# An mLSTM and soft-MoE kernel: q and k tiles on 128 partitions, gate rows as 4096-byte rows, and a newly written instruction order

## The chip, the cores and the metric

The kernel runs on one core of a Trainium2 chip. The metric is the device time of one execution in microseconds (us); lower is better.

## The reference, cut to what matters

The input has 4 batches, 8 heads, 768 positions and 40 values per head. First comes a gated linear attention with a running state per head, written as a recurrence in time:

```
m_new = max(f_gate + m, i_gate); f_stab = exp(f_gate + m - m_new); i_stab = exp(i_gate - m_new)
C = f_stab * C + i_stab * outer(v, k);  n = f_stab * n + i_stab * k
y = sigmoid(o_gate) * (C q) / max(|n.q|, 1)
```

Its result, as 3072 rows of 320 values, goes through one feed-forward layer and then through a soft mixture of experts:

```
h = x @ w_in;  x = (h * sigmoid(h)) @ w_out              # 320 -> 2048 -> 320
logits = x @ phi;  d = softmax of logits over the 3072 rows (per slot, 32 slots)
slot_input = d.T @ x;  per expert e (8): slot_out = relu(slot_input[e] @ w1[e]) @ w2[e]     # 320 -> 1024 -> 320
c = softmax of logits over the 32 slots;  out = c @ slot_out
```

## The kernel before, in words

The recurrence is computed in chunks. A tile is 128 positions of one batch with all 8 heads; there are 24 tiles, and two tiles make a block of 256 rows, of which there are 12. For each tile the kernel loads q and k (`load_qk`), k and v in rows (`load_v`), the gate rows (`rows`, from the scratch tensor `md` in device memory) and, for two tiles at once, the output gate (`load_o`). TensorE then makes the scores (`sc`, L610), the state update (`st`, L643) and the output (`pv`, L669), and turns the output round (`xT`, L689). `qs` multiplies q by a gate row into `xq`; `mask`, `arg` and `exp` make the decay weights; `vw` weighs v. Each block goes through the feed-forward layer in eight steps (`mlp.blk.q`: 16 matmuls at L716, then a Silu on ScalarE at L718), and its hidden values are turned by VectorE (`gU`, L725) into two tiles named `g`. The logits (`lg`, L735; `lsum`, L747) and the slot sums (`slots`, L775, two steps of 32 matmuls, one for each `g` tile of the block) follow.

Ahead of this, the weights `w_in` (`load_wi`, `load_wr`) and `w_out` (`load_wo`) come in a 64-bit layout and are converted on ScalarE and VectorE (`wi`, `wr`, `wo`); the converted `w_out` is turned round and multiplied by phi (`wpT`, L450; `wp`, L462). After the last block come the slot inputs (`slot_in`), the two expert layers (`s1`, L932, which needs all tiles of `w1`; `s2`, L959, which needs `w2`) and the output (`out`, L977, and its transfers at L981). The steps `warm` and `heat` are matmuls whose results nobody reads.

The order of all work is the string `ORDER`: a list of 1416 tokens such as `mlp.3.6` or `load_w2.2.3`. Each token issues the next step of the operation it names; each engine works through its steps strictly in this order. `ENG` says which engine does a step that several could do. All loads but those of the last stage's output go through the one queue of SyncE, also in this order: a load that must wait for its buffer holds up all loads behind it.

Memory is reused. The tiles of the attention lie in a pool that `free_at` closes, and 10 of the 20 tiles of `w1` are then loaded over it. Five more are loaded into the common buffers `cv` in the earlier blocks. The tiles of the feed-forward layer lie in a pool that `free_mp` closes, and the 32 tiles of `w2` (320 KB each) and the last five of `w1` (512 KB each) are loaded over that. By the code, that pool holds per partition eight weight tiles of 4096 bytes, `wr` with 8192, `gT` with 16384, then the four buffers of `g` with 8192 bytes each (at 57344, 65536, 73728 and 81920), then the block's inputs. The tile `w2_e_k` lies at byte (8k + e) x 2560, so `load_w2.2.3` (e = 2, k = 3) at 66560 lies in the second buffer of `g`, `load_w2.6.3` at 76800 in the third, and the first tile of `load_w1.6` at 81920 in the fourth:

```
for k in range(4):
    for e in range(NE):
        w2t[e, k] = yp.tile([128, 2, DM], F32, name=f"w2_{e}_{k}")
for e, c in ((6, 0), (6, 1), (6, 2), (7, 0), (7, 1)):
    w1t[e, c] = yp.tile([128, F2], F32, name=f"w1_{e}_{c}")
```

A load into such a tile waits only for the readers of what lay there.

Of the kernel before, what the change touches and what calls it, by code (L numbers as in the profile page):

```python
# [78 lines left out]
load_wo.4 xT.0 wi.3 wi.3 pv.1 load_v.2 vw.2 xT.0 xT.0 st.2 rows.2 pv.1 pv.1 xT.1 wi.3 wi.3 wo.4 xT.1 xT.1 mlp.0.0 wo.4 wo.4 load_wo.0 load_wo.2 sdec.1.1
load_wo.3 wi.3 wo.2 wo.2 wo.0 wo.0 wo.2 wo.0 sadd.1.1 wo.3 wo.3 mask.2 arg.2 exp.2 wo.3 decay.0 mlp.0.0 mlp.0.5 mlp.0.5 load_qk.2 sc.2 sw.2 load_wo.1 wo.1  # L80
wo.1 wo.1 decay.0 load_wo.14 wo.14 wo.14 wo.14 load_wo.7 wo.7 wo.7 wo.7 mlp.0.2 mlp.0.2 load_wo.13 wo.13 wo.13 wo.13 load_wo.6 wo.6 wo.6 wo.6 wpT.1 wpT.0
mlp.0.4 mlp.0.4 mlp.0.7 mlp.0.6 load_wo.15 wo.15 wo.15 load_wo.5 wpT.0 wo.15 wo.5 wo.5 wo.5 wpT.1 load_wo.12 wo.12 wo.12 wo.12 mlp.0.7 load_wo.10 wpT.3 wo.10
wo.10 wpT.2 mlp.0.6 wpT.3 wo.10 sdec.2.0 sadd.2.0 load_wo.11 wo.11 wo.11 wpT.2 mlp.0.3 load_p load_wo.9 wo.9 wo.9 wo.9 load_wo.8 wo.8 wo.8 wo.8 wo.11 wpT.6
wpT.6 wpT.7 mlp.0.1 wpT.7 load_v.3 mlp.0.1 sdec.2.1 wpT.4 wpT.4 mlp.0.3 wpT.5 wpT.5 qs.2 pv.2 mask.3 gU.0.0 load_o.1 sadd.2.1 sdec.3.0 wz.0 wpT.8 vw.3 wz.1
gU.0.0 wpT.9 sig.1 wpT.8 wpT.9 st.3 sadd.3.0 pv.2 rows.3 arg.3 exp.3 sdec.3.1 sadd.3.1 gU.0.1 pv.2 pv.2 wp load_qk.3 wp sc.3 sw.3 qs.3 xT.2 xT.2 wp wp
load_qk.4 sc.4 xT.2 pv.3 pv.3 pv.3 lg.0 mask.4 load_v.4 vw.4 pv.3 xT.3 st.4 gU.0.3 lg.0 load_o.2 lsum.0 xT.3 xT.3 rows.4 arg.4 exp.4 sw.4 mlp.1.0 mlp.1.0
load_v.5 lsum.0 vw.5 mlp.1.1 rows.5 mlp.1.1 qs.4 sdec.4.0 sadd.4.0 pv.4 sig.2 lsum.0 row.0 gU.0.1 mlp.1.2 mlp.1.2 mlp.1.5 gU.0.2 pv.4 load_v.6 gU.0.2 mlp.1.5
pv.4 row.0 gU.1.0 lsum.0 load_qk.5 qs.5 mlp.1.4 sdec.4.1 gU.0.3 pv.4 sadd.4.1 mlp.1.4 xT.4 xT.4 mlp.1.6 mlp.1.6 gU.1.0 mask.5 st.5 sdec.5.0 sadd.5.0 arg.5
exp.5 sc.5 gU.1.2 sw.5 lsum.0 mlp.1.7 mlp.1.7 mlp.1.3 mlp.1.3 vw.6 init row.0 pv.5 pv.5 xT.4 pv.5 pv.5 lg.1 lg.1 row.0 row.0 slots.0 load_qk.6 rows.6 sdec.6.0
mask.6 xT.5 rows.8 xT.5 load_v.7 load_w1.0 load_w1.0 slots.0 arg.6 exp.6 xT.5 mlp.2.1 mlp.2.1 mlp.2.3 gU.1.1 gU.1.1 slots.0 slots.0 slots.0 slots.0 row.0  # L90
# [982 lines left out]
```

## Time and profile before

| what | us |
|---|---|
| time, median of 3 runs | 413.08 (411.52 to 414.05) |
| time of the profiled execution | 412.9 |
| its span, first to last instruction | 411.1 |
| PE busy in the span | 388.4 (94%) |
| DVE, ACT, POOL busy | 247.3, 241.1, 119.9 |

The span is what the trace covers; the rest of the time lies around it. Engines: PE is the TensorE matmul, PEld its weight load, DVE is VectorE, ACT is ScalarE, POOL is GpSimd, and SPq is the queue of loads on SyncE.

### The profile page before, as it was taken

What the parts mean: (1) busy time and instruction counts of PE and PEld (TensorE: products, weight loads), DVE (VectorE), ACT (ScalarE), POOL (GpSimd) and SP (SyncE); (2) the same over time, 40 slices, a digit from 0 to 9 for tenths busy, and PEclk for the clock granted to TensorE, in tenths of its full rate; (3) what the DMA queues carried; (4) which work ended last, traced back from release to release, by engine and by line L of the source; (5) the groups of instructions that cost most, each with busy time, mean ns of one, the idle gap of its engine ahead of it and who ended that gap; (6) DMA issues with size and microseconds to landing.
All of it is one profiled execution on the core that took longest, in us unless ns stands there. A gap on an engine that the chain in (4) does not pass through costs nothing.

```text
span 411.1 us, 14943 instructions
## 1 busy us (share of the span) xinstructions
PE 388.4 (94%) x6526; PEld 316.9 (77%) x6526; DVE 247.3 (60%) x569; ACT 241.1 (59%) x475; POOL 119.9 (29%) x169
## 2 busy tenths in 40 slices
...
GB/s 255 346 260 281 232 274 226 117 214 216 250 78 237 155 84 157 164 104 172 167 195 57 127 70 242 111 157 183 157 96 65 77 357 290 204 279 364 227 135 251
DMA packets 36992, 78.43 MB, mean 191 GB/s; under 512 B 3616, under 2 KB 18656, under 8 KB 36288
## 3 DMA queue, kind: packets, MB, share of 16 engines
...
## 4 chain that ended last, share of the span: by engine, by line
PE 74%; DMA 15%; DVE 3%; SPq 3%; issue 2%; ACT 1%; POOL 1%; DVEq 0%; ACTq 0%; POOLq 0%
PE h L716 39%; DMA w<-in_moe_w 6%; PE w L669 5%; PE t L735 5%; PE w L775 5%; DMA qk<-in_qk 5%; PE w L610 3%; PE w L643 3%; PE t L959 3%; DMA mq<-md 2%; PE t L689 2%; PE h L238 2%; PE t L395 1%; DMA cv<-in_moe_w_out 1%; PE t L747 1%
## 5 line engine op out<-in xcount | busy, mean ns | idle before, releaser
L718 ACT ACTIVATE gT<-h 128x512 f32<-128x512 f32 x96 | 56.4, 598 | 63.3 <-PE h L716 59.2
L716 PE MATMUL h<-xh,wh 128*128 128x256 f32 x384 | 83.0, 298 | 1.0 <-ACT gT L718 1.0
L716 PE MATMUL h<-xl,wh 128*128 128x256 f32 x384 | 77.4, 283 | 0.0
L716 PE MATMUL h<-xh,wl 128*128 128x256 f32 x384 | 77.3, 283 | 0.0
L725 DVE STREAM_TRANSPOSE g<-gT 128x512 f32<-128x512 f32 x96 | 63.5, 690 | 12.6 <-ACT gT L718 12.6
L716 PEld LDWEIGHTS h<-xh,wh 128*128 128x128 f32 x384 | 59.4, 191 | 11.7 <-issue 3.4
L716 PEld LDWEIGHTS h<-xh,wl 128*128 128x128 f32 x384 | 59.7, 191 | 0.0
L716 PEld LDWEIGHTS h<-xl,wh 128*128 128x128 f32 x384 | 59.6, 191 | 0.1
L716 PE MATMUL h<-xh,wr 128*128 128x256 f32 x192 | 54.3, 283 | 0.0
L716 PE MATMUL h<-xl,wr 128*128 128x256 f32 x192 | 54.2, 282 | 0.0
L594 POOL TENSOR_TENSOR xq<-qk,mq 104x512 f32<-104x512 f32 x20 | 25.7, 1286 | 44.6 <-ACT mq L303 16.3
L779 DVE SCALAR_TENSOR_TENSOR acc<-acc,vec,w 128x512 f32<-128x512 f32 x44 | 30.1, 737 | 11.6 <-PE w L775 11.6
L716 PEld LDWEIGHTS h<-xl,wr 128*128 128x128 f32 x192 | 36.8, 192 | 0.0
L716 PEld LDWEIGHTS h<-xh,wr 128*128 128x128 f32 x192 | 36.8, 192 | 0.0
L718 ACT ACT_TABLE_LOAD x27 | 34.6, 1283 | 1.9 <-DVE g L725 1.4
L570 POOL TENSOR_TENSOR arg<-mq,arg 128x512 f32<-128x512 f32 x17 | 22.8, 1339 | 20.1 <-DVE arg L564 11.8
L775 PE MATMUL w<-g,et 32*32 32x512 f32 x768 | 27.4, 600 | 0.1
L654 DVE TENSOR_TENSOR vb<-vb,w 104x164 f32<-104x164 f32 x40 | 12.6, 314 | 24.1 <-PE w L643 17.0
L669 PE MATMUL w<-vb,xq 40*64 40x41 f32 x768 | 24.4, 227 | 1.2 <-issue 1.2
L669 PE MATMUL w<-kv,xs 64*64 64x41 f32 x768 | 24.9, 229 | 0.0
L618 DVE TENSOR_TENSOR xs<-w,arg 128x512 f32<-128x512 f32 x24 | 16.4, 683 | 13.2 <-ACT arg L575 6.6
L669 PEld LDWEIGHTS w<-kv,xs 64*64 64x64 f32 x768 | 20.7, 133 | 4.4 <-issue 1.8
...
## 6 DMA issues: line engine op xcount, KB each, us to landing
...
rawi<-in_moe_w_in SPq DMA_DIRECT2D x4, 1024.0 KB, 12.0
...
```

Source lines behind the costliest of these rows:

```text
L570: eng(f"arg.{n}", "G" if n else "V").tensor_tensor(out=arg, in0=mb.rearrange("p r (c t) -> p r c t", c=2), in1=arg, op=ALU.add)
L594: eng(f"qs.{n}", "G").tensor_tensor(out=xq[LR], in0=qkt[n % 2][LR, 0:4], in1=st[n]["qb"][LR], op=ALU.mult)
L610: T_.matmul(sc[64 * z:64 * z + 64, y, f:f + 64], qkn[o:o + D, 4 + p, t], qkn[o:o + D, 8 * y + x, t], start=True, stop=True, tile_position= ...
L618: V_.tensor_tensor(out=h2(d["xs"]), in0=d["sc"], in1=h2(d["arg"]), op=ALU.mult)
L654: V_.tensor_tensor(out=dst, in0=dst, in1=u, op=ALU.add)
L669: T_.matmul(op[64 * ch:64 * ch + 64, NP * par + p], a, vv[k][r, ch, p], start=(k == 0), stop=(k == 1), tile_position=(o, 64 * ch))
L716: T_.matmul(hp[:, z], w, x, start=(y == 0), stop=(y == 7))
L718: A_.activation(out=gt[0][:, 2 * q:2 * q + 2], in_=hp, func=AF.Silu)
L725: V_.transpose(out=us[blk][a][:, :, 4 * q:4 * q + 4].rearrange("p b c f -> p c b f"), in_=gt[0][:, 4 * q:4 * q + 4, 128 * a:128 * a + 128] ...
L735: T_.matmul(lp[32 * j:32 * j + 32], wp[:, j, 32 * q:32 * q + 32], gt[0][:, 4 * q + j], start=(q == 0), stop=(q == 3), tile_position=(0, 32 ...
L775: T_.matmul(ap[g][32 * b:32 * b + 32], d["et"][p, 4 * a + b], u[p, b].rearrange("p c f -> p (c f)"), start=(a == 0), stop=(a == 1), tile_p ...
L779: V_.scalar_tensor_tensor(out=acc[:, g], in0=acc[:, g], scalar=al[:, blk:blk + 1], in1=ap[g], op0=ALU.mult, op1=ALU.add)
```

## The change

Four things change, and no step is added or taken away: both orders hold the same 1416 tokens, each as often.

- q and k are loaded on 128 partitions, where it was 112 before (partitions 40 to 63 and those from 104 on hold zeros): 640 KB instead of 560 KB a tile.
- `md` lies so that the two gate rows of a pair of heads stand side by side. The two transfers of `rows` stay two, each to 64 partitions and of 256 KB, but a partition's data is one row of 4096 bytes where it was two of 2048. The tile `mq` is laid out likewise, so its readers read runs of 128 values with a step.
- The pads behind the rows of `qk` and `kv` in device memory are gone.
- `ORDER` and `ENG` are written anew, for the buffers as the program builds them.

```diff
-DP = 112
+DP = 128
...
-load_f scan first load_c keys keys mask.0 rest first load_o.0 sig.0 decay.1 prow.1 prow.1 rest rest rest load_wr wr wr wr mb0 rest decay.1 decay.1 wr wr
...
-free_at load_w1.4 load_w1.4 pv.23 load_w1.4 load_w1.2 mlp.10.5 mlp.10.5 row.9 row.9 row.9 mlp.10.2 mlp.10.2 gU.10.1 xT.23 mlp.10.4 slots.9 load_w1.2 load_w1.2
...
-lsum.10 lsum.10 load_w1.3 mlp.11.0 mlp.11.0 gU.11.0 free_mp load_w2.1.0 mlp.11.3 mlp.11.3 load_w2.0.0 lsum.10 load_w2.2.0 mlp.11.2 load_w2.4.0 mlp.11.2
-load_w2.3.0 row.9 row.9 row.10 load_w2.5.0 gU.10.3 gU.10.2 gU.10.3 mlp.11.7 mlp.11.7 gU.11.0 lsum.10 slots.10 load_w1.6 mlp.11.6 load_w2.2.1 load_w1.6
-mlp.11.6 gU.11.3 mlp.11.5 row.10 gU.10.2 mlp.11.5 mlp.11.4 mlp.11.4 load_w2.3.1 row.10 load_w1.7 gU.11.1 gU.11.1 gU.11.2 slots.10 load_w2.2.3 lg.11 lg.11
-slots.10 slots.10 slots.10 lg.11 lg.11 lg.11 lsum.11 load_w2.7.0 slots.10 lsum.11 heat.6 load_w2.4.1 load_w1.6 lsum.11 load_w1.7 heat.2 load_w2.7.1
-load_w2.5.1 lsum.11 lsum.11 slots.11 load_w2.6.3 before before load_w2.4.3 gU.11.2 gU.11.3 slots.11 load_w2.6.2 load_w2.4.2 load_w2.6.1 load_w2.2.2
-load_w2.1.2 load_w2.3.3 load_w2.0.1 heat.5 load_w2.5.3 load_w2.0.3 row.10 row.10 row.10 row.10 load_w2.0.2 load_w2.5.2 slots.11 slots.11 slots.11 slots.11
...
-s1.1 s1.1 s1.1 hT.0 hT.0 hT.0 hT.1 row.11 row.11 load_w2.6.0 row.11 load_w2.7.2 s2.1 hT.1 hT.1 load_w2.1.1 s2.1 s2.1 s2.0 s2.1 load_w2.3.2 s2.1 load_w2.1.3
-load_w2.7.3 s2.1 s2.1 s2.1 s2.0 s2.0 s2.1 out.6.1 out.6.1 out.6.1 out.1.1 out.1.1 out.1.1 out.0.1 out.0.1 s2.0 out.5.1 out.5.1 out.5.1 row.11 row.11 out.0.1
...
+init load_v.1 load_f scan rest first load_c keys first qb0 keys mask.0 decay.1 decay.1 first warm.0.6 load_wr wr wr wr wr wr wr qb0 ws.1 ws.1 load_wi.0 wi.0
...
+xT.22 pv.23 pv.23 lsum.9 free_at load_w1.2 load_w1.3 load_w1.3 load_w1.4 row.9 xT.22 row.9 row.9 mlp.10.4 pv.23 pv.23 load_w1.2 load_w1.2 xT.22 mlp.10.4
...
+gU.10.1 lsum.10 row.9 mlp.11.0 mlp.11.1 mlp.11.1 lsum.10 gU.11.0 gU.11.0 mlp.11.7 mlp.11.7 row.9 load_w1.4 slots.9 load_w1.4 slots.9 free_mp load_w2.1.0
+load_w1.5 load_w2.0.0 mlp.11.6 load_w2.2.1 mlp.11.6 load_w2.2.0 load_w2.3.1 mlp.11.3 gU.11.3 mlp.11.3 mlp.11.2 mlp.11.2 mlp.11.4 gU.11.1 gU.11.1 load_w2.3.0
+load_w2.5.0 load_w2.4.0 mlp.11.5 load_w2.5.1 row.9 load_w2.6.0 load_w1.7 lsum.10 load_w2.7.0 lsum.10 slots.10 mlp.11.4 row.9 row.10 gU.11.3 row.10 mlp.11.5
+gU.11.2 load_w2.4.1 gU.11.2 row.10 lg.11 slots.10 load_w2.6.3 load_w2.1.1 slots.10 load_w2.0.1 load_w1.6 load_w1.6 slots.10 slots.10 lg.11 lg.11 lg.11
+load_w2.2.2 lg.11 lsum.11 lsum.11 lsum.11 load_w2.1.2 load_w1.6 load_w2.6.1 load_w1.7 slots.10 heat.7 lsum.11 lsum.11 heat.5 load_w2.0.2 slots.11 load_w2.2.3
+load_w2.4.3 load_w2.4.2 row.10 row.10 before before slots.11 load_w2.1.3 load_w2.0.3 heat.3 slots.11 row.10 slots.11 slots.11 load_w2.7.2 slots.11 slot_in
...
+row.11 row.11 row.11 s1.0 s1.1 hT.0 hT.0 hT.0 s1.1 s1.1 load_w2.5.2 s2.1 s2.1 hT.1 hT.1 hT.1 load_w2.7.1 s2.1 load_w2.5.3 s2.1 s2.0 load_w2.3.2 load_w2.6.2
+load_w2.3.3 s2.1 s2.0 load_w2.7.3 s2.1 s2.1 s2.1 s2.1 s2.0 out.4.1 out.4.1 out.4.1 out.3.1 out.3.1 row.11 row.11 out.3.1 out.2.1 out.2.1 out.2.1 s2.0 out.5.1
...
-    md = tc.dram_tile([2, 2, NR, 128], F32, name="md")
+    md = tc.dram_tile([2, NR, 2, 128], F32, name="md")
...
-        d = md[i % 2]
-        n = d.shape[1]
-        a = d[:, 2 * NP * (b * NQ + i // 2) + NP * par]
-        return bass.AP(a.tensor, a.offset, [[0, 64], [128 * n, 2], [1, 128 * NP]])
+        a = md[i % 2, 2 * NP * (b * NQ + i // 2) + NP * par]
+        return bass.AP(a.tensor, a.offset, [[0, 64], [1, 256 * NP]])
...
-        Y_.dma_start(out=qkt[n % 2][0:DP].rearrange("p a t -> p (a t)"), in_=qk[n, :, 0:1280])
+        Y_.dma_start(out=qkt[n % 2], in_=qk[n])
...
-        Y_.dma_start(out=kvt[n % 2], in_=kv[n, :, 0:DM + 2 * H * (D + 1)])
+        Y_.dma_start(out=kvt[n % 2], in_=kv[n])
...
-        mq = work([128, 2, NP, 128], "mq")
+        mq = work([128, NP, 2, 128], "mq")
         for par in range(2):
-            Y_.dma_start(out=mq[64 * par:64 * par + 64].rearrange("p x a t -> p x (a t)"), in_=bcast(b, i, par))
-        st[n].update(mb=mq[:, 0], qb=mq[:, 1])
+            Y_.dma_start(out=mq[64 * par:64 * par + 64].rearrange("p a x t -> p (a x t)"), in_=bcast(b, i, par))
+        st[n].update(mb=mq[:, :, 0], qb=mq[:, :, 1])
```

The other lines of the two orders place the same steps in another sequence.

## Rows read from the trace of the kernel before

**Rows 1.** Busy time by stretch: length, PE, PEld, DVE, ACT, POOL, granted clock, DMA, GB/s.
```profile
0.00:80.00 80.00, 68.52 (x991) 54.36 (x992) 55.16 (x115) 50.72 (x90) 27.75 (x37) 1.00 0.86 256
80.00:355.00 275.00, 273.20 (x4958) 234.28 (x4960) 175.18 (x415) 177.19 (x348) 87.98 (x124) 1.00 0.55 162
```
**Rows 2.** The same view, of the last stage.
```profile
353.00:361.00 8.00, 7.26 (x119) 3.56 (x122) 6.23 (x14) 3.78 (x11) 0.00 (x0) 1.00 0.40 145
361.00:386.00 25.00, 19.73 (x206) 7.80 (x202) 4.75 (x14) 6.00 (x19) 3.69 (x7) 0.98 1.01 348
386.00:389.00 3.00, 3.00 (x56) 2.19 (x52) 0.00 (x0) 0.00 (x0) 0.00 (x0) 0.58 0.23 82
389.00:394.00 5.00, 5.00 (x129) 4.27 (x120) 0.72 (x2) 0.05 (x1) 0.00 (x0) 1.00 0.02 6
```
**Rows 3.** Timeline of PE, last stage: start, us, line, shapes, count, idle before.
```profile
345.92 1.14 PE L775 MATMUL w<-g,et 32*32 32x512 f32 x32
...
359.39 1.15 PE L775 MATMUL w<-g,et 32*32 32x512 f32 x32
...
361.48 1.15 PE L775 MATMUL w<-g,et 32*32 32x512 f32 x32
...
371.40 0.63 PE L932 MATMUL h<-w,wo 128*32 128x512 f32 x3
...
381.76 0.49 PE L959 MATMUL t<-w,wo 128*32 128x168 f32 x6 [0.21 <-ACT wo L948]
385.77 7.64 PE L959 MATMUL t<-w,wo 128*32 128x168 f32 x170 [3.52 <-DMA w<-in_moe_w]
...
397.15 1.76 PE L959 MATMUL t<-w,wo 128*32 128x152 f32 x48
```
**Rows 4.** Timeline of the SyncE queue, last stage: loads of w1 (L848) and w2 (L852).
```profile
325.39 7.47 SPq L848 DMA_DIRECT2D w<-in_moe_w  x10
...
347.24 0.34 SPq L848 DMA_DIRECT2D w<-in_moe_w  x1
...
352.96 0.34 SPq L848 DMA_DIRECT2D w<-in_moe_w  x1
360.71 1.39 SPq L852 DMA_DIRECT2D w<-in_moe_w  x3
362.15 0.94 SPq L848 DMA_DIRECT2D w<-in_moe_w  x2
363.13 20.28 SPq L852 DMA_DIRECT2D w<-in_moe_w  x21
```
**Rows 5.** Waits of the SyncE queue from 345 to 362: us in total, times, longest.
```profile
SPq L852 <- PE w L775: 6.3, 1, 6.3
```
**Rows 6.** The chain that ended last: start, us, what; sixty-four matmuls are four steps.
```profile
336.20 7.67 PE h L716 x64
```
**Rows 7.** Timeline of PE at the start: the first matmul.
```profile
5.55 1.09 PE L277 MATMUL t<-gb 96*64 96x48 f32 x16 [5.55 <-DMA gb<-in_const]
```
**Rows 8.** Timeline of the SyncE queue at the start.
```profile
27.53 0.34 SPq L352 DMA_DIRECT2D md<-gb  x1
```
**Rows 9.** Waits of PE from 55 to 80: us in total, times, longest.
```profile
PE t L450 <- ACT wt L227: 1.4, 1, 1.4
PE w L669 <- issue: 1.2, 1, 1.2
PE w L610 <- DMA qk<-in_qk: 1.1, 1, 1.1
PE t L450 <- DVE wo L377: 0.6, 1, 0.6
```
**Rows 10.** The tile qk: its 24 loads of 560 KB, from issue to landing.
```profile
DMA to landing us min/median/max: 4.2/7.5/14.9
```
**Rows 11.** The tile kv: its 24 loads of 488 KB.
```profile
DMA to landing us min/median/max: 3.5/4.9/12.2
```
**Rows 12.** The tile og: its 12 loads of 320 KB.
```profile
DMA to landing us min/median/max: 2.9/6.5/10.8
```

More of the change, by code (lines that the diff above doesn't have):

```diff
@@ L79 @@
[L79 to L90, printed above, removed]
@@ L91 @@
-row.0 row.0 st.6 gU.1.3 sc.6 sw.6 mlp.2.7 vw.7 mlp.2.3 sadd.6.0 qs.6 pv.6 load_o.3 gU.1.3 sig.3 mlp.2.7 pv.6 sdec.6.1 sadd.6.1 mlp.2.0 mlp.2.0 gU.2.0 gU.2.0
-mlp.2.2 rows.7 mask.7 arg.7 exp.7 load_o.4 load_w1.1 mlp.2.2 lsum.1 lsum.1 lsum.1 load_qk.7 qs.7 row.1 sc.7 st.7 mlp.2.6 sdec.7.0 sadd.7.0 sdec.7.1 sw.7
-gU.1.2 pv.6 mlp.2.5 pv.6 mlp.2.6 xT.6 sadd.7.1 row.1 sdec.8.0 pv.7 mask.8 pv.7 arg.8 sig.4 lsum.1 lsum.1 load_qk.8 sc.8 exp.8 sw.8 xT.6 xT.6 gU.2.3 mlp.2.5
-mlp.2.4 pv.7 pv.7 xT.7 mlp.2.4 xT.7 slots.1 row.1 lg.2 lg.2 slots.1 rows.9 load_o.6 gU.2.2 mask.9 xT.7 mlp.3.6 mlp.3.1 gU.2.3 arg.9 qs.8 gU.2.1 load_v.8
@@ L115 @@
-mlp.7.7 xT.17 xT.17 lg.7 slots.6 slots.6 mlp.8.3 row.6 row.6 row.6 row.6 gU.7.2 lg.7 exp.18 slots.6 slots.6 slots.6 mlp.8.2 mlp.8.2 load_v.18 row.6 row.6
-mlp.8.3 load_qk.18 sc.18 sw.18 vw.18 st.18 lsum.7 sadd.18.0 gU.7.3 gU.7.3 qs.18 load_qk.19 load_v.19 pv.18 sig.9 pv.18 pv.18 pv.18 mlp.8.1 mlp.8.1 mlp.8.0
-mlp.8.0 vw.19 st.19 sdec.18.1 sadd.18.1 sdec.19.0 mask.19 rows.19 arg.19 exp.19 qs.19 sc.19 xT.18 xT.18 lsum.7 gU.7.2 load_o.10 lsum.7 lsum.7 load_w1.0
-load_v.20 vw.20 xT.18 mlp.8.6 mlp.8.6 sadd.19.0 mlp.8.5 mlp.8.5 sw.19 sdec.19.1 sadd.19.1 sdec.20.0 pv.19 pv.19 load_v.21 pv.19 pv.19 st.20 sadd.20.0 mask.20
@@ new lines @@
+wpT.9 pv.2 sdec.3.1 load_o.1 sig.1 pv.2 pv.2 sadd.3.1 load_p wp wp load_qk.3 sc.3 arg.3 exp.3 sw.3 pv.2 mlp.0.2 xT.2 wp wp qs.3 pv.3 pv.3 load_v.4 vw.4 st.4
+xT.2 xT.2 mlp.0.5 gU.0.2 lg.0 pv.3 pv.3 xT.3 load_qk.4 lg.0 sc.4 sdec.4.0 sadd.4.0 sdec.4.1 lsum.0 xT.3 xT.3 gU.0.1 gU.0.1 mlp.1.0 gU.0.0 mlp.1.0 load_o.2
+sig.2 gU.0.2 rows.4 qs.4 mask.4 sadd.4.1 mlp.1.5 lsum.0 mlp.1.5 lsum.0 row.0 arg.4 exp.4 sw.4 mlp.1.4 mlp.1.4 mask.5 mlp.1.6 row.0 gU.0.3 gU.0.3 mlp.1.6
+load_qk.5 load_v.5 sc.5 pv.4 sdec.6.0 mlp.1.1 pv.4 pv.4 mlp.1.1 gU.1.0 rows.6 gU.1.0 sdec.5.0 pv.4 vw.5 mlp.1.3 mlp.1.3 mlp.1.7 mlp.1.2 st.5 lsum.0 rows.5
@@ new lines @@
+qs.5 lsum.0 load_qk.7 arg.5 exp.5 init row.0 mlp.1.2 xT.4 xT.4 sw.5 sadd.5.0 pv.5 pv.5 pv.5 load_qk.6 qs.6 mlp.1.7 gU.1.2 lg.1 lg.1 xT.4 slots.0 pv.5 gU.1.1
+gU.1.1 xT.5 xT.5 row.0 row.0 lsum.1 xT.5 slots.0 slots.0 lsum.1 slots.0 slots.0 slots.0 mlp.2.2 mlp.2.2 mask.6 arg.6 exp.6 mlp.2.0 load_v.7 load_v.6 vw.6 st.6
+vw.7 mlp.2.0 lsum.1 load_w1.1 sc.6 gU.1.3 sadd.6.0 row.0 mlp.2.3 mlp.2.3 gU.1.3 rows.7 mlp.2.1 mlp.2.1 load_o.3 sig.3 load_qk.8 sw.6 sdec.6.1 sadd.6.1
+sdec.7.0 mask.7 arg.7 lsum.1 exp.7 sc.7 pv.6 pv.6 pv.6 qs.7 pv.6 lsum.1 sw.7 row.0 row.0 mlp.2.7 mlp.2.5 mlp.2.7 gU.1.2 mlp.2.5 st.7 sadd.7.0 sdec.7.1 mlp.2.4
@@ new lines @@
+gU.2.0 gU.2.1 mlp.2.4 gU.2.2 sadd.7.1 sdec.8.0 gU.2.2 row.1 mlp.2.6 xT.6 mlp.2.6 pv.7 row.1 pv.7 rows.8 mask.8 arg.8 exp.8 sc.8 sw.8 row.1 row.1 xT.6 xT.6
+pv.7 pv.7 load_v.8 mask.9 vw.8 lg.2 slots.1 load_w1.1 row.1 row.1 lg.2 xT.7 lsum.2 gU.2.1 lsum.2 load_w1.0 lsum.2 xT.7 xT.7 slots.1 slots.1 gU.2.3 gU.2.3
+load_qk.9 load_o.4 lsum.2 lsum.2 rows.9 arg.9 exp.9 mlp.3.6 mlp.3.6 slots.1 mlp.3.2 slots.1 st.8 gU.2.0 sadd.8.0 slots.1 sdec.8.1 sadd.8.1 mlp.3.0 qs.8
+load_qk.10 pv.8 sig.4 mlp.3.2 pv.8 pv.8 sc.9 sw.9 mlp.3.1 sdec.9.0 qs.9 row.1 row.1 slots.2 load_v.9 vw.9 pv.8 xT.8 slots.2 mlp.3.1 mlp.3.0 mask.10 rows.10
@@ new lines @@
+mlp.3.4 slots.2 slots.2 slots.2 gU.3.0 slots.2 arg.10 exp.10 mlp.3.4 xT.8 st.9 sadd.9.0 sdec.9.1 sadd.9.1 mlp.3.5 mlp.3.5 pv.9 pv.9 qs.10 load_v.10 vw.10
+sc.10 sw.10 mlp.3.3 mlp.3.3 load_w1.0 load_w1.0 rows.11 load_qk.11 xT.8 mlp.3.7 pv.9 pv.9 xT.9 row.2 st.10 load_o.7 sdec.10.0 row.2 gU.3.0 xT.9 xT.9 mlp.3.7
+lg.3 lg.3 sadd.10.0 pv.10 row.2 gU.3.1 sdec.10.1 sadd.10.1 sdec.11.0 gU.3.1 mlp.4.1 load_qk.12 load_o.5 sig.5 mlp.4.1 gU.3.3 row.2 row.2 mask.11 arg.11
+sdec.12.0 pv.10 mlp.4.2 mlp.4.2 load_v.11 vw.11 gU.3.2 gU.3.2 row.2 lsum.3 st.11 sc.11 gU.3.3 mlp.4.7 row.2 row.2 mlp.4.7 mlp.4.4 lsum.3 lsum.3 sadd.11.0
@@ new lines @@
+exp.11 lsum.3 rows.12 pv.10 pv.10 mlp.4.0 xT.10 mlp.4.4 load_v.12 vw.12 st.12 sw.11 qs.11 pv.11 load_qk.13 sadd.12.0 lsum.3 sdec.12.1 mlp.4.0 gU.4.0 qs.12
+sadd.12.1 pv.11 pv.11 sdec.13.0 pv.11 xT.10 xT.10 gU.4.0 mlp.4.3 mlp.4.3 gU.4.1 mlp.4.5 mlp.4.5 slots.3 xT.11 xT.11 xT.11 row.3 mlp.4.6 row.3 slots.3 slots.3
+slots.3 mlp.4.6 gU.4.3 gU.4.2 slots.3 gU.4.3 lg.4 lg.4 row.3 row.3 slots.3 sc.12 mask.12 arg.12 exp.12 sw.12 mlp.5.1 mlp.5.1 rows.13 mask.13 arg.13 load_o.6
+mlp.5.0 sig.6 mlp.5.0 gU.4.2 load_qk.14 lsum.4 lsum.4 lsum.4 pv.12 load_v.14 load_v.13 gU.4.1 sc.13 exp.13 pv.12 pv.12 pv.12 sw.13 mlp.5.4 mlp.5.5 lsum.4
@@ new lines @@
+lsum.4 gU.5.0 qs.13 row.3 load_qk.15 rows.14 slots.4 mlp.5.4 xT.12 xT.12 slots.4 mlp.5.3 slots.4 slots.4 slots.4 row.3 row.3 vw.13 mlp.5.5 st.13 row.3
+sadd.13.0 sdec.13.1 slots.4 mlp.5.2 mlp.5.3 mlp.5.2 row.4 xT.12 sig.7 pv.13 mlp.5.6 pv.13 sadd.13.1 gU.5.1 gU.5.1 pv.13 pv.13 mlp.5.6 load_v.15 mlp.5.7
+mlp.5.7 xT.13 sdec.14.0 gU.5.0 mask.14 arg.14 row.4 xT.13 xT.13 gU.5.2 qs.14 row.4 row.4 sc.14 vw.14 st.14 vw.15 exp.14 gU.5.3 sw.14 row.4 lg.5 lg.5 gU.5.2
+mlp.6.5 mlp.6.5 gU.5.3 sadd.14.0 mlp.6.0 mlp.6.0 lsum.5 lsum.5 pv.14 sdec.14.1 lsum.5 lsum.5 row.4 row.4 row.4 mlp.6.1 pv.14 mlp.6.3 rows.16 rows.15 mask.15
@@ new lines @@
+arg.15 exp.15 row.5 lsum.5 pv.14 pv.14 xT.14 mlp.6.1 row.5 sadd.14.1 qs.15 sdec.15.0 sc.15 load_qk.17 rows.21 load_v.16 mlp.6.3 sw.15 xT.14 xT.14 st.15
+sadd.15.0 gU.6.0 mask.16 sdec.15.1 sadd.15.1 mlp.6.2 mlp.6.2 gU.6.1 mlp.6.7 mlp.6.6 row.5 row.5 pv.15 load_v.17 pv.15 pv.15 mlp.6.7 mlp.6.6 gU.6.3 gU.6.3
+arg.16 mlp.6.4 pv.15 xT.15 mlp.6.4 slots.5 lg.6 slots.5 load_qk.16 qs.16 row.5 row.5 xT.15 xT.15 gU.6.2 mlp.7.6 mlp.7.6 slots.5 slots.5 lg.6 mlp.7.0 slots.5
+slots.5 gU.6.0 vw.16 sc.16 st.16 sdec.16.0 sadd.16.0 exp.16 sdec.16.1 sadd.16.1 sdec.17.0 mlp.7.0 mlp.7.1 mlp.7.1 gU.6.1 sw.16 mlp.7.2 row.5 lsum.6 gU.6.2
```

81 lines of the change are left out of this document (36 added, 45 removed), and 54 rows, old and new, of the table ENG.

## Prediction

> **What bounds the kernel now.** I read the busy time by stretch first. From 80 to 355 us PE is busy 273.2 of 275 us at a granted clock of 1.00, while DMA is busy 0.55 and VectorE 175 of 275 [rows 1]. The reader is to see that here the matmuls alone set the time, and since both orders hold the same matmuls, this stage has 1.8 us to give and no more. What the change can win lies at the two ends: in the first 80 us PE is idle for 11.5 us [rows 1], and after 355 us the loads of the last stage come into the way.
>
> Then the last stage. From 361 to 386 us DMA is full (1.01, 348 GB/s), but from 353 to 361 it was busy only 0.40 [rows 2]. The timeline of the SyncE queue says why: after the load issued at 352.96 nothing is issued until 360.71, and then 26 loads follow at once (3, 2 and 21) [rows 4]. In the old order the load behind the one at 352.96 is `load_w2.2.3`. Its 6.3 us of waiting are put down to L775 [rows 5], and it goes 0.17 us after the end of a step of `slots` that begins at 359.39 and takes 1.15 [rows 3]: the first step of `slots.11`. The old order has it directly behind the second step of `slots.10`, and about half of the loads that stand behind it (those with k = 0 and 1, the rest of w1, and those in the third buffer of `g`) read no place that was still in use. The 26 loads, 24 of 320 KB and 2 of 512 KB, are 8.9 MB, 25.6 us at 348 GB/s: 360.7 + 25.6 = 386.3, and PE in fact waits for a load of w2 until 385.77, when 170 matmuls of L959 can start; the first six had started at 381.76 [rows 3]. [...]
>
> **The last stage, changed.** The new order does not place the same load behind the same step. Which buffer holds what can be read off the old trace: the first tile of `load_w1.6` lies in the fourth buffer of `g` and was issued at 347.24, as the first step of `slots.10` (345.92 + 1.14) ended [rows 3, 4]; `load_w2.2.3`, in the second, was let go by the first step of `slots.11`. So the four are used backwards: third by the second step of `slots.10`, first by the second of `slots.11`. The new order fits that: `load_w2.6.3` (third buffer) and `load_w1.6` behind the steps of `slots.10`, `load_w2.2.3` behind the first of `slots.11`, `load_w2.1.3` behind the second. I went through the other loads in the same way, by the offsets in the code; each stands behind the last `mlp.11`, `lg.11` or `gU.11` that reads its place.
>
> Then only DMA's own pace counts. Behind `free_at` stand 15 loads of 512 KB and 32 of 320 KB, 18.35 MB, 52.7 us at 348 GB/s. They begin when `pv.23` lets the attention's tiles go, at 325.39 in the old trace [rows 4]; the new order has one `mlp` step more ahead of that, 7.67 / 4 = 1.9 us [rows 6]. A load takes some 2.1 us beyond its transfer (kv at its fastest: 3.5 less the 1.4 of 488 KB at that rate [rows 11]; an estimate), and I allow 1.5 us for two places where the queue must wait for an `mlp.11` step: 325.4 + 1.9 + 52.7 + 1.5 + 2.1 = 383.6, all landed by 384. PE reaches `s2` at 381.76 as before, but doesn't need all then: a step of 16 matmuls takes 1.76 / 3 = 0.59 us [rows 3], and tiles with k = 3 are first read by the ninth step of `s2`, behind `hT.1` too, near 387. The k = 2 and k = 1 tiles end 2 and 5 loads earlier in the queue and are read near 385.5 and 384. For `s1` at 371.40 the last tile of w1 stands 14 loads ahead of the end, 13 us earlier, so at 371, and is read only in the fourth of its five rounds. So the wait goes: 385.77 - 381.76 = 4.0, less 0.2 for the pause that remains. The slow clock behind it goes with it: 56 matmuls took 3.0 us from 386 to 389, and at the 129 in 5.0 of the next stretch [rows 2] they take 2.2, with 0.3 for the stretch before 386, 1.1 us. **Term: -4.9 us**, bounds -5.5 and -1.5 (the DMA end 3.4 us later than worked out). What is late next is PE itself: `s2` and `out` follow as before, with the same four or five `heat` steps at the end.
>
> **The start.** The new order issues `load_v.1`, 488 KB, ahead of the gates and constants, which the first matmul waits for until 5.55 [rows 7]. That costs at least one issue (0.45) and at most its whole transfer, 1.4 us at 348 GB/s; I take 1.0, since the small loads behind it were not transfer-bound. The second store to `md` (27.53 [rows 8]) needs two POOL steps and two ScalarE steps that the new order has put behind `arg.1` and `exp.1`; behind it on the SyncE queue stand `rows.2` and 15 of the 16 loads of w_out. Counting the steps in front of it I get about 30, later by 2.5 us; PE has `w_in` and eight `mlp.0` steps to do meanwhile, so I price it from 0 to 2.5 and take 1.2, in the middle. Against this stand four waits of PE between 55 and 80 us: 1.4, 1.2, 1.1 and 0.6, 4.3 in all [rows 9], of which two hang on the w_out conversion and two on tile 3 and 4 loads that queue behind the last w_out loads. The new order has one of these tile loads behind `wp`, and starts its `wpT` groups as soon as four tiles are converted; I take half back, 2.2. **Term: 0**, bounds 1.0 - 4.3 = -3.3 and 1.4 + 2.5 = +3.9, of which I keep +3.
>
> **The middle.** Of the 1.8 us I take back 0.5; upward +2, as much again as all waits there are now, since ENG gives VectorE four more of the `og` steps and four more `qs`, on engines that are busy two thirds at most [rows 1]. From the positions of loads and readers the shortest time from the earliest issue of a load to its first reader is 2.0 us in the old order (`load_qk.7`) and 5.6 in the new (`load_v.9`); nearest price of such a load: 3.5 at least, 4.9 in the median [rows 11]. **Term: -0.5**, bounds -1.8 and +2.
>
> **q and k on 128 partitions, rows of 4096 bytes.** A q and k tile grows by 80 KB. From og to kv a load takes 0.6 us more for 168 KB [rows 11, 12], so 80 KB are 0.3 us; from kv to qk it is 0.7 for 72 KB [rows 10, 11], 0.8 us for 80. At either price it is hidden under matmuls except where PE waits for qk (1.1 [rows 9]), so 0 to +0.8, taken as 0 within the two terms above. That qk costs so much more per byte than kv is in the rows; the difference is 112 partitions against 128. [...] The gate rows keep their bytes and their two transfers; half as many rows can only save, by an amount that no row gives, and nothing on PE's path hangs on it at present: 0. Readers of `mq` step over 128 values: VectorE and POOL have the room [rows 1], 0.
>
> **Sum.** -4.9 + 0 - 0.5 = -5.4. On the profiled execution 412.9 - 5.4 = 407.5; that execution is 0.2 below the median, so 407.7 on the median of 413.08. About 1%, 4.1 us, is what a measurement can tell from no change.
>
> **Rivals.**
> - The start gives its waits back too. All four waits go and the early load costs little, -3.0 more: 404.7. For it: POOL idles in the first 80 us for over half of them [rows 1], so the moved steps may cost nothing. Against: ScalarE and VectorE are the ones that convert.
> - The start pays. The later store holds up w_out, the conversion ends 2.5 to 3 us later, and PE waits at `wp`: 407.7 + 2.8 = 410.5. For it: the load behind which PE waits is then in a DMA stretch that is 0.86 full [rows 1].
> - Slower: the tile loads become PE's bound in the middle. 24 loads of q and k grow by up to 0.8 us each, on a queue where each waits for the reader of its buffer two tiles earlier. Where a load has no time to spare, PE waits at `sc` (L610), as it did once for 1.1 us [rows 9]. With half of the tiles, 12 x 0.8 = 9.6: 417.3. It decides from 7 tiles on (5.4 / 0.8). Against it: the shortest distance of 5.6 us above, against 4.2 for qk at its fastest [rows 10].
> - The order doesn't do what it says, and the buffers are not used as I read them: the queue stops again. If the third buffer of `g` is let go only by the second step of `slots.11` (361.48 + 1.15 [rows 3]), `load_w2.6.3` waits until 362.6; the last tile of w1 is the tenth load from there (6 of 320 KB, 4 of 512 KB, 11.7 us), lands at 362.6 + 11.7 + 2.1 = 376.4, and is first read in the fourth round of five of the first half of `s1`, 3/10 of the way from 371.40 to 381.76 [rows 3], so at 374.5: 1.9 us of waiting, and 0.3 for the w2 tiles behind it: 407.7 + 2.2 = 409.9.
>
> **Chances.** Forecast (406 to 409.5) 0.45; start gives back 0.20; start pays 0.18; the queue stops again 0.10; slower 0.07. Faster than 408.95 are four fifths of the first case and all of the second, 0.56; half of the last reaches beyond 417.2, 0.04; the rest, 0.40, lies within 1%. The range 403.5 to 413 holds the first four with what their bounds add: 1.2 below the second for the middle's remaining 1.3 us, 2.5 above the third and fourth for the middle's 2.
>
> **What would show it.** The SyncE queue without a gap from 325 to the last load of w2; no idle of PE at L959 of more than 0.5 us and a clock of 1.00 to the end of `s2`. First matmul at 6.0 to 7.0. PE idle before 80 us of 9 to 14. DMA to landing of qk near 4.2 at the least. Wrong would be: a second gap in the queue, a wait at L450 or L462 above 2 us, or waits at L610 and L716 in the middle that sum to over 2 us.

## The result, and the profile after

| kernel | median us | of runs | against the kernel before, 95% interval |
|---|---|---|---|
| after | 406.78 (405.23 to 407.87) | 4 | 0.9863 [0.9816, 0.9911] |
| before, beside it | 412.70 (411.52 to 414.05) | 4 | 1 |

The change gains 5.9 us by the medians, 1.4% by the ratio; the forecast was 407.7. Two later measurements of the same kernel, in experiments 5 and 9 to 12, give ratios of 0.9806 and 0.9776, that is 8.0 and 9.2 us; the three intervals overlap. The profiled execution of the kernel after is its fastest, 405.2 us with a span of 403.4; by the two profiled spans the gain is 411.1 - 403.4 = 7.7. Ratios here and below leave out disturbed executions, medians take all. Line numbers of the kernel after are 2 less than before from L524 on; where a kernel below has an order with tokens moved, they are 3 more than that from `ORDER` on.

The same stretches as [rows 1] and [rows 2], with the same columns:

```profile
0.00:80.00 80.00, 65.80 (x991) 52.60 (x992) 53.06 (x115) 51.97 (x92) 25.88 (x37) 0.96 0.82 268
80.00:355.00 275.00, 274.47 (x4972) 234.58 (x4971) 185.46 (x438) 179.82 (x349) 82.53 (x106) 1.00 0.53 167
353.00:361.00 8.00, 7.26 (x109) 3.45 (x102) 4.31 (x12) 2.13 (x8) 0.46 (x1) 1.00 1.01 370
361.00:386.00 25.00, 23.62 (x328) 12.20 (x326) 5.84 (x19) 5.95 (x18) 2.37 (x2) 1.00 0.78 273
386.00:389.00 3.00, 3.00 (x43) 2.58 (x47) 1.31 (x2) 2.24 (x7) 0.46 (x1) 1.00 0.31 93
```

In the last stage DMA is full from 353 to 361, where it was at 0.40; PE is idle for 1.4 us from 361 to 386, where it was 5.3, and the granted clock stays at 1.00. The middle is idle for 0.5 us, where it was 1.8. The first 80 us have become worse by this view: 14.2 us idle against 11.5, and a clock below 1.00. That holds for this execution; in another of the same kernel (experiment 5) it is 10.2 us idle at a clock of 1.00.

The timeline of PE, last stage, against [rows 3]:

```profile
357.23 1.15 PE L773 MATMUL w<-g,et 32*32 32x512 f32 x32
...
369.23 0.62 PE L930 MATMUL h<-cv,wo 128*32 128x512 f32 x1 [0.20 <-DVE wo L913]
...
380.40 5.18 PE L957 MATMUL t<-w,wo 128*32 128x168 f32 x144
385.94 0.57 PE L975 MATMUL h<-so,cT 128*128 128x168 f32 x3 [0.37 <-DVE so L963]
```

The two rows that [rows 3] doesn't show, from the kernel before:

```profile
371.39 0.62 PE L932 MATMUL h<-cv,wo 128*32 128x512 f32 x1 [0.45 <-DVE wo L915]
...
393.34 0.57 PE L977 MATMUL h<-so,cT 128*128 128x168 f32 x3
```

From the first step of `s1` (369.23) to the first of `out` (385.94) it is 16.7 us; before it was 393.34 - 371.39 = 21.95. The wait of 3.5 us for a tile of `w2` is gone, and 144 matmuls take 5.18 us where 170 took 7.64. The queue of SyncE, against [rows 4]:

```profile
325.11 4.23 SPq L846 DMA_DIRECT2D w<-in_moe_w  x9
337.67 0.38 SPq L850 DMA_DIRECT2D w<-in_moe_w  x1
...
350.88 3.26 SPq L850 DMA_DIRECT2D w<-in_moe_w  x5
354.19 1.54 SPq L846 DMA_DIRECT2D w<-in_moe_w  x2
356.74 1.23 SPq L850 DMA_DIRECT2D w<-in_moe_w  x2
358.49 0.34 SPq L846 DMA_DIRECT2D w<-in_moe_w  x1
```

Between 350.4 and the last load no stop is longer than 1.5 us. There is a stop ahead of 337.67, where `w2` waits 7.9 us for a feed-forward step that still reads its place. The kernel before has it too, between the ten loads from 325.39 on in [rows 4] and this row, which [rows 4] leaves out:

```profile
339.82 6.02 SPq L852 DMA_DIRECT2D w<-in_moe_w  x6
```

The waits of PE in the first 80 us (total, times, longest), against [rows 7] and [rows 9]:

```profile
PE t L277 <- DMA gb<-in_const: 7.5, 1, 7.5
PE t L395 <- DVE cv L377: 2.5, 2, 2.1
PE w L608 <- DMA qk<-in_qk: 1.5, 1, 1.5
PE t L687 <- ACT wl L398: 1.1, 1, 1.1
PE h L714 <- ACT gT L716: 1.0, 1, 1.0
PE w L641 <- POOL vz L581: 0.2, 1, 0.2
```

The four waits between 55 and 80 us are gone but for 0.2 us. Others have come up between 17 and 48 us, 6.1 in all, where the kernel before has 1.5 ahead of 55. Both differ from execution to execution: the one of experiment 5 has 2.5 us in place of the 6.1, and that of experiments 9 to 12 has again a wait of 1.8 us between 55 and 80 (at L667).

### The profile page after: what moved, and what is told of

Its sections match the earlier page's. It is cut to its first block, busy times and chain, and to the rows that moved or that the text cites. A ratio compares the mean times of both kernels' runs of the same rounds, so it can differ in the third digit from the quotient of the medians.

```text
span 403.4 us, 14925 instructions
## 1 busy us (share of the span) xinstructions
PE 383.8 (95%) x6526; PEld 313.9 (78%) x6526; DVE 253.3 (63%) x590; ACT 244.7 (61%) x478; POOL 111.7 (28%) x147
## 4 chain that ended last, share of the span: by engine, by line
PE 86%; DMA 6%; ACT 3%; DVE 2%; SPq 1%; issue 1%; POOL 0%; ACTq 0%; DVEq 0%
PE h L714 47%; PE w L773 6%; PE w L667 6%; PE t L733 6%; PE w L641 3%; PE w L608 3%; PE h L930 2%; PE t L687 2%; PE t L957 2%; DMA rawi<-in_moe_w_in 2%; DMA rawr<-in_moe_w_in 2%; PE t L745 1%; DMA cv<-in_moe_w_out 1%; PE t L516 1%; DMA kv<-in_kv 1%; ACT cv L370 1%
## 5 line engine op out<-in xcount | busy, mean ns | idle before, releaser
L592 POOL TENSOR_TENSOR xq<-qk,mq 104x512 f32<-104x512 f32 x16 | 20.8, 1303 | 38.0 <-PE w L667 19.9
L568 POOL TENSOR_TENSOR arg<-mq,arg 128x512 f32<-128x512 f32 x18 | 23.9, 1326 | 21.2 <-DMA mq<-md 14.4
L562 POOL TENSOR_TENSOR arg<-con,ahp 128x512 f32<-128x512 f32 x18 | 20.3, 1126 | 21.1 <-DVE xs L616 20.9
L667 PE MATMUL w<-kv,xs 64*64 64x41 f32 x768 | 24.6, 229 | 0.0
L667 PE MATMUL w<-vb,xq 40*64 40x41 f32 x768 | 24.3, 227 | 0.0
L667 PEld LDWEIGHTS w<-kv,xs 64*64 64x64 f32 x768 | 20.6, 133 | 4.0 <-issue 1.8
L733 PE MATMUL t<-gT,wp 128*32 128x256 f32 x384 | 23.5, 382 | 0.0
```

Source lines behind the costliest of these rows:

```text
L562: eng(f"mask.{n}", "G").tensor_tensor(out=arg, in0=mk, in1=av.unsqueeze(3).to_broadcast([128, NP, 2, 64]), op=ALU.subtract)
L568: eng(f"arg.{n}", "G" if n else "V").tensor_tensor(out=arg, in0=mb.rearrange("p r (c t) -> p r c t", c=2), in1=arg, op=ALU.add)
L592: eng(f"qs.{n}", "G").tensor_tensor(out=xq[LR], in0=qkt[n % 2][LR, 0:4], in1=st[n]["qb"][LR], op=ALU.mult)
L667: T_.matmul(op[64 * ch:64 * ch + 64, NP * par + p], a, vv[k][r, ch, p], start=(k == 0), stop=(k == 1), tile_position=(o, 64 * ch))
L733: T_.matmul(lp[32 * j:32 * j + 32], wp[:, j, 32 * q:32 * q + 32], gt[0][:, 4 * q + j], start=(q == 0), stop=(q == 3), tile_position=(0, 32 ...
```

## The experiments

The theory taken from the prediction: the stop of the SyncE queue is worth about 5 us, the start and the layouts nothing. Rivals: the layouts carry part of it; the start does; the last stage gains by something else in the new order.

**1. The stop taken out of the old order.**

```diff
-slots.10 load_w2.2.3 lg.11
+slots.10 lg.11
-slots.11 load_w2.6.3
+slots.11 load_w2.2.3 load_w2.6.3
```

> The kernel before, with one token moved: load_w2.2.3 from behind the second step of slots.10 to behind the first step of slots.11. Theory (the stop of the SyncE queue makes the wait in the last stage): six loads go in the gap from 353 to 361 us, the other twenty follow at once and have landed by 382, the wait at L959 falls from 3.5 us to under 0.5, the granted clock stays at 1.00 from 386 to 389, and the time falls by 4 to 5.5 us against the kernel before. Rival (DMA is too slow for the last stage whatever the order): the wait at L959 stays above 2 us and the time falls by less than 2.

Measured: 408.12 us (7 runs) beside 411.77 for the kernel before (26 runs), 0.9909 [0.9877, 0.9941], so 3.7 us by the ratio [2.4, 5.1], a little under the 4 to 5.5 that were expected, and 5.0 by the spans behind `slots.11` (table below). The view by stretch, the PE timeline at `s2` and the queue:

```profile
353.00:361.00 8.00, 7.26 (x117) 3.52 (x119) 6.09 (x14) 3.72 (x10) 0.00 (x0) 1.00 0.98 342
361.00:386.00 25.00, 23.25 (x316) 11.31 (x312) 4.89 (x15) 6.05 (x19) 3.69 (x7) 1.00 0.87 298
386.00:389.00 3.00, 3.00 (x75) 2.66 (x67) 0.72 (x2) 0.15 (x1) 0.00 (x0) 1.00 0.03 5
```
```profile
381.99 6.32 PE L962 MATMUL t<-w,wo 128*32 128x168 f32 x176 [0.20 <-ACT wo L951]
```
```profile
353.19 0.34 SPq L851 DMA_DIRECT2D w<-in_moe_w  x1
353.59 0.94 SPq L855 DMA_DIRECT2D w<-in_moe_w  x2
354.58 1.12 SPq L851 DMA_DIRECT2D w<-in_moe_w  x2
355.74 21.70 SPq L855 DMA_DIRECT2D w<-in_moe_w  x22
```

One token moved, and the queue runs on at 353.59, the 176 matmuls of `s2` go without a wait for a load, and the clock does not fall. The mechanism holds.

**2. A stop put into the new order.**

```diff
-slots.10 load_w2.6.3
+slots.10 load_w2.1.3 load_w2.6.3
-slots.11 load_w2.1.3
+slots.11
```

> The kernel after, with one token moved the other way: load_w2.1.3, whose buffer is let go by the second step of slots.11, directly behind the second step of slots.10. Theory: the SyncE queue stands from about 351.8 to 360.5 us, 24 loads (8.65 MB, 24.9 us at 348 GB/s) then land by 385 to 387, where the tiles with k = 3 are first read near 383.6: a wait of 1.5 to 4 us at L957 comes back, with a granted clock below 0.9 behind it, and the time is 2.5 us (1.5 to 4.5) above that of the kernel after. Rival (the tail gained by something else in the new order, such as s1 and s2 overlapping): within 1 us of the kernel after.

Measured: 409.20 us (12 runs), 0.9917 [0.9875, 0.9959]. Against the three ratios of the kernel after (0.9863, 0.9806, 0.9776) the stop costs 2.2, 4.6 or 5.8 us, each give or take some 2.6; the spans behind `slots.11` (table below), which leave out the start, say 4.6 to 4.8. The queue stands until the second step of `slots.11` ends (356.68 + 1.15) and goes on at 358.03, so the buffers are used as the prediction reads them:

```profile
358.03 1.39 SPq L853 DMA_DIRECT2D w<-in_moe_w  x3
```

The waits of PE from 345 us on:

```profile
PE h L933 <- DMA w<-in_moe_w: 3.0, 1, 3.0
...
PE t L960 <- DMA w<-in_moe_w: 0.4, 1, 0.4
```

A wait came back, and the price by the spans is just above the upper end of what was expected (4.5), but the wait is at another place: `s1` (L933) misses the last tile of `w1`, which stood behind the stop too, and `s2` hardly waits. The granted clock stayed at 1.00, against the expectation.

**3 and 4. Layouts and order apart.** The old ORDER and ENG with the new layouts, and the new ones with the old layouts.

> The old ORDER and ENG with the three changes of layout (q and k on 128 partitions, gate rows of 4096 bytes, no pads). Theory of the prediction: 0 against the kernel before, within 1.5 us, and a q and k tile lands in 4.2 us or less at its fastest although it carries 640 KB. Rival (the layout costs what its bytes cost): up to 0.8 us for each exposed load, 1 to 3 us slower. Other rival (128 partitions spread the transfer better, and the short waits for qk go): 1 to 2 us faster.

> The new ORDER and ENG with the old layouts. Theory: all of the gain is in the order, so 5 to 6.5 us faster than the kernel before, within 1 us of the kernel after. Rival: the layouts carry 1 us or more of the gain, and this kernel is 1 us or more slower than the one after; the landing of qk, 560 KB on 112 partitions, then has a median above 5.8 us under the same order.

Measured: old order with new layouts 408.96 us (11 runs), 0.9934 [0.9898, 0.9970], 2.7 us faster than before. New order with old layouts 408.38 us (9 runs), 0.9902 [0.9861, 0.9943]; against the three ratios of the kernel after the layouts are worth 1.6, 4.0 or 5.2 us there, each give or take some 2.6. So they carry some 3 to 4 us, in either order; the old order has the better evidence, with an interval of 1.2 to 4.2 us. The theory that they are worth 0 has fallen. The sign that the second expectation named for it, a median landing of qk above 5.8 us, was hardly there (5.9); it shows in DMA's time instead, as experiment 8 does.

**5, 6 and 7. The start.** The kernel after once more, and one move in each order:

```diff
 (old order, warm early)
-load_f scan first load_c keys keys mask.0 rest first load_o.0
+init load_f scan first load_c keys keys mask.0 rest first warm.0.6 load_o.0
-sw.0 init warm.0.6 load_wi.1
+sw.0 load_wi.1
 (new order, kv later)
-init load_v.1 load_f scan rest first load_c keys
+init load_f scan rest first load_c load_v.1 keys
```

> The kernel after, unchanged, beside the others of this call. Both theories: 0.986 of the kernel before, 5 to 6.5 us faster. With it the layouts' share (new order with new layouts against new order with old layouts, 0.9902) can be read from the same number of runs: theory that the layouts carry part of the gain, 1 to 3 us below that kernel; rival that they carry none, within 1 us.

> The kernel before, with init and the twelve matmuls of warm ahead of the first gate work of PE instead of behind the first product at L396. Theory (what the start gains is the earlier rise of TensorE's clock): the 32 matmuls of L238 that begin at 13.22 us and take 3.68 us take about 2.1, the 32 of L610 0.67 instead of 1.14, mlp.0.0 begins 1 to 3 us earlier, and the time falls by 1 to 3 us. Rival (the start hangs on the loads of w_in and their conversion): the matmuls are shorter, but PE then waits at L395 for cv, and mlp.0.0 begins within 0.5 us of 38.9; the time is within 1 us of the kernel before.

> The kernel after, with load_v.1 behind the gates and constants instead of ahead of them. Theory (the early kv load costs the start about 1 us): the first matmul at 5.5 to 6.0 us instead of 7.5, and the time falls by 1 to 2 us. Rival (the first matmul is not what the start hangs on, since PE waits at L395 near 19.6 for the conversion of w_in): the first matmul is earlier, the wait at L395 longer by as much, and the time is within 1 us of the kernel after.

Measured beside 412.76 us for the kernel before (17 runs): the kernel after 404.62 (6 runs, 402.67 to 408.22), 0.9806 [0.9758, 0.9854]; kv later 405.17 (6), 0.9802 [0.9751, 0.9854]; warm early 413.21 (12), 0.9988 [0.9952, 1.0024]. In the kernel with kv later the first matmul goes at 5.30 instead of 7.52 us, and nothing comes of it: PE then waits 2.4 us for `mq` at L241, where the kernel after has no wait. The early load of kv costs no time that can be seen. With `warm` early, PE and the clock by stretch and on the timeline:

```profile
10.00:15.00 5.00, 4.44 (x54) 3.79 (x52) 2.95 (x7) 2.42 (x4) 0.00 (x0) 0.91 1.04 286
15.00:20.00 5.00, 5.00 (x63) 4.13 (x60) 4.14 (x5) 4.57 (x8) 0.91 (x1) 0.50 1.02 406
```
```profile
12.57 1.09 PE L241 MATMUL h<-gb,con 96*64 96x128 f32 x16
...
14.11 3.68 PE L241 MATMUL h<-gb,con 96*64 96x128 f32 x32
17.73 1.13 PE L613 MATMUL w<-qk 40*64 40x64 f32 x32
```

Sixteen matmuls at 12.57 take 1.09 us, where the kernel before takes 1.98 for as many of the same form at 10.38; 1.5 us later the same instruction is slow again (3.68 us for 32), most of it in a stretch at a granted clock of 0.50. The faster pace came early and was not kept; `mlp.0.0` begins at 39.41 where it was 38.90, and the time didn't change. So this run doesn't say what a higher clock that stays would be worth.

**8. q and k on 128 partitions alone**, in the old order, with the pads and the old gate rows.

```diff
-DP = 112
+DP = 128
```

> The kernel before, with q and k on 128 partitions alone; pads and gate rows stay as they were. Theory (the partitions make the transfer better): the landing of qk is 4.0 us or less at its fastest, DMA moves over 380 GB/s from 10 to 15 us where it was 279, and the time falls by 1.5 to 3 us, as with all three layouts. Rival (the gate rows of 4096 bytes and the missing pads make the gain): qk lands no earlier than before, and the time is within 1 us of the kernel before or above it.

Measured: 408.97 us (6 runs), 0.9895 [0.9857, 0.9933]. The page's DMA queue (packets, MB, share of 16 engines), before and here:

```profile
q1 hardware_dynamic: 35328, 76.55, 61.9%
```
```profile
q1 hardware_dynamic: 35712, 78.52, 58.7%
```

Its windows, after a row of the kernel before, and the landing of qk (560 KB in [rows 10], 640 KB here):

```profile
10.00:15.00 5.00, 5.00 (x39) 4.21 (x41) 3.33 (x6) 2.77 (x4) 0.00 (x0) 1.00 1.01 279
```
```profile
0.00:80.00 80.00, 69.80 (x1058) 55.41 (x1058) 57.82 (x118) 51.80 (x92) 28.32 (x37) 1.00 0.77 261
10.00:15.00 5.00, 5.00 (x38) 4.21 (x39) 3.29 (x6) 2.71 (x4) 0.00 (x0) 1.00 1.01 420
```
```profile
DMA to landing us min/median/max: 3.5/6.8/10.7
```

More bytes go in less time: 0.619 x 16 x 411.1 = 4072 us of DMA engines' time before, 0.587 x 16 x 407.1 = 3824 here, 6% less for 2.6% more bytes; from 10 to 15 us, at a full DMA in both, 420 GB/s where the kernel before has 279. In the single packets of the traces, one of qk (5120 bytes, a partition's row) takes 296 ns in the median before and 196 in the kernel after, which has q and k on 128 partitions too. This one edit is worth 4.3 us [2.8, 5.9], no less than all three layouts (2.7). For gate rows and pads no gain can be seen.

**9 to 12. The two causes together, and a better start.**

```diff
 (old order, new layouts, and the move of experiment 1)
 (new order, load_wi.3 early)
-load_qk.1 sc.1
+load_qk.1 load_wi.3 sc.1
-rest rest load_wi.3 rest
+rest rest rest
 (the same with two more steps that nobody reads)
-sc.0 wi.0
+sc.0 heat.8 heat.9 wi.0
```

> The old ORDER and ENG with the new layouts and with load_w2.2.3 behind the first step of slots.11. Theory (two causes make all of the gain: the layouts 0.989 to 0.993, the stop of the queue 0.991): 0.981 to 0.985 of the kernel before, 6.5 to 8 us faster, and as fast as the kernel after within 1 us. Rival (the rest of the new order carries 2 us or more): 2 us or more slower than the kernel after beside it.

> The kernel after, unchanged, as the mark for the others of this call: 0.980 to 0.987 of the kernel before. Its runs should be ordered by their granted clock, as in the call before (402.67 us at 1.00, 408.22 at 0.978).

> The kernel after, with load_wi.3 directly behind load_qk.1, where it stood behind the first store to md. Theory (the start hangs on the loads of w_in and w_out, which stand behind md): it is issued near 12 us instead of 24 to 25, DMA's hole from 20 to 25 us is filled, the wait at L395 near 30 us and those for wl and gT up to 48 us go, mlp.1.0 begins 1 to 2 us earlier and the time falls by 1 to 2 us. Rival (the four buffers of w_in and the conversion set the pace): within 1 us of the kernel after.

> The kernel of the run before, with two more steps of heat (four matmuls whose results nobody reads) behind sc.0, where PE waits 0.6 to 2.1 us at L395. Theory (the wait there makes the granted clock fall from 20 to 25 us): the clock stays at 1.00 up to 40 us, and the slowest runs come nearer to the fastest: median 1 us below the kernel without them. Rival (PE is late there as often as it waits): they cost their 1 us or so, 0 to 1 us slower.

Measured beside 412.80 us (11 runs), with 6 runs of each:

| kernel | median us | ratio |
|---|---|---|
| old order, both causes | 405.58 | 0.9826 [0.9765, 0.9886] |
| after | 405.07 | 0.9776 [0.9714, 0.9839] |
| after, load_wi.3 early | 403.87 | 0.9760 [0.9694, 0.9826] |
| the same with two steps of heat | 402.98 | 0.9749 [0.9703, 0.9796] |

The old order with the new layouts and one token moved is as fast as the kernel after by the medians; by the ratios up to 2 us may be left for the rest of the new order, and the intervals overlap. The last kernel has the lowest median, 2.1 us below the kernel after beside it, but the intervals overlap, and I don't call it faster. With `load_wi.3` early the load goes at 12.97 us instead of 25.31, and DMA is busy 0.77 from 20 to 25 us where it was 0.27, as expected; but `mlp.0.0` doesn't begin earlier (41.58 against 37.08 to 39.23 in three executions of the kernel after), so that the expected way to the gain isn't there. With the two steps of `heat` the clock is 1.00 from 10 to 50 us, as expected. Of the six executions of the kernel after, the two at a granted clock of 1.00 are the shortest, 400.35 and 400.87 us.

## Why the prediction was right in the sum and wrong in a term

The spans of the profiled executions, cut at the first step of `slots.11` (its start in the PE timeline; the rest is the span less that start), us:

| kernel | to slots.11 | from there |
|---|---|---|
| before | 359.39 | 51.7 |
| old order, stop taken out | 359.62 | 46.7 |
| old order, new layouts | 356.53 | 51.1 |
| old order, qk on 128 alone | 356.07 | 51.0 |
| old order, warm early | 358.73 | 51.5 |
| old order, both causes | 358.81 | 46.6 |
| new order, old layouts | 361.18 | 46.3 |
| after (three executions) | 357.23, 354.53, 357.30 | 46.2, 46.4, 46.3 |
| new order with a stop | 354.59 | 51.0 |
| new order, kv later | 357.75 | 46.4 |
| after, load_wi.3 early | 355.53 | 46.2 |
| the same with two steps of heat | 354.97 | 46.3 |

- **The last stage, -4.9: right.** The right column has two values, 46.2 to 46.7 and 51.0 to 51.7, and which one a kernel gets hangs on the place of one token (`load_w2.2.3` in the old order, `load_w2.1.3` in the new). The kernel after gains 5.5, at the bound of -5.5; the wait and the slow clock behind it (0.58 from 386 to 389 in [rows 2], 1.00 in the kernel after) went, as worked out. Not right was that SyncE would have no gap from 325 us on: it stands for 8 us ahead of 337.67, and for as long again in pieces up to 350, where I had allowed 1.5. The old trace has a stop of 7 us at the same place (332.86 to 339.82), which I passed over. DMA was through earlier than the 383.6 of the sum all the same, near 379.5. While the queue stood it had loads in hand (first row); only in the pieces after that did it run below its rate (second row):

```profile
328.00:337.00 9.00, 9.00 (x137) 6.27 (x136) 5.03 (x10) 3.94 (x10) 0.00 (x0) 1.00 1.02 412
337.00:352.00 15.00, 15.00 (x178) 13.02 (x176) 9.25 (x22) 8.71 (x14) 0.00 (x0) 1.00 0.83 272
```

  The fast stretch makes up for the slow one: 18.35 MB in 54.4 us less the 2.1 of a landing are 351 GB/s, against the 348 of the sum, and the 1.5 us were not needed. The other 2.2 us are an earlier start, 325.11 for 327.3: counted back from `slots.11` the first load is 1.9 us later than before, as worked out (32.1 us ahead of it against 34.0), but all work ahead of it was over 2.2 us sooner.
- **The queue stops again, 409.9: it did not come about.** Experiment 2 makes a like stop by another load, and there the mechanism is right and the size is not. The tile that is missed is the last of `w1`, as that rival had it and my expectation for the run did not; it costs 3.4 us of waiting and 4.6 to 4.8 of time by the spans, where the rival had 2.2.
- **q and k on 128 partitions, 0: wrong, and the step that failed.** I priced 80 KB more by the rows of smaller loads, at 0 to +0.8 us for each load, and took it as hidden. The price has the other sign: 4.3 us less [2.8, 5.9] for this edit alone. Where it went in the old order can be read in part: the waits for qk at L610 (1.1 in [rows 9], 0.8 more further on) are not in the list of waits any more, and the kernel is ahead by 1.6 us at the first step of `slots.0` (96.27 against 97.85), by 2.4 at that of `slots.1` (121.36 against 123.79) and by 3.3 at that of `slots.11`. The first 1.6 us are no safe sign, since the old order with `warm` early is ahead by 1.9 there (96.00) and gains nothing in time. The row that should have told me stood in the prediction, that qk costs more per byte than kv; I put it down as a fact of 112 partitions and did not ask what 128 would give back. In the traces a tile of 640 KB lands in 3.8 us at the least in the kernel after and in 3.5 in experiment 8, one of 560 KB in 4.2 before. Why 112 partitions are slow was not shown.
- **The start, 0: about right as a sum, wrong inside.** The first matmul came at 7.52, not between 6.0 and 7.0, but that was not a price: moving the load back brought the matmul forward and no time. PE is idle for 14.2 us before 80, just over the 9 to 14 of the forecast. The four waits of 55 to 80 us went but for 0.2 in this execution, not by half (one of them, L669, has `issue` in its row, so that I had put it down to a load without evidence), and 6.1 us of others came up ahead of them. The second store to `md` went at 29.43, near the 30 worked out. I had missed the clock: the 32 matmuls of L238 that took 3.68 us before take 2.08 after, behind `warm`, which the new order has ahead of them, and the clock is at 0.70 from 20 to 25 us. What that is worth is open: with `warm` early in the old order the matmuls were faster too (1.09 us for 16 at 12.57), and slow again when those 32 came (3.68 us, the clock at 0.50).
- **The middle, -0.5: right in sign, -1.3 by the idle time.** The waits for qk (0.8) and gT (1.0) that the kernel before has there are gone.
- **The sum: inside the range, and in part by luck.** By the two profiled spans the change gives 7.7 us, 5.5 from `slots.11` on and 2.2 ahead of it, where the sum had 4.9 and 0.5. By the ratio it gives 5.7, 8.0 and 9.2 us in three measurements, and the forecast of 5.4 lies near the first alone. The layouts were worth 3 to 4 us more than I said. By the spans they gave 1 to 7 us ahead of `slots.11` (358.81 against 359.62 at the least, 354.53 against 361.18 at the most); what the new order itself does there lies between a loss (361.18 with the old layouts against 359.39) and a small gain (354.53 with the new ones against 356.53), and the scatter of the start, 2.8 us between three executions of one kernel, hides it. This stays open.
